# A three-layer fp32 kernel on one core: score matmuls on all four quarters of the array, another opening order, earlier loads and later stores of the first MLP's activations

## The chip, the core and the metric

The kernel runs on one core of a Trainium2 chip. TensorE (PE) multiplies matrices and writes to PSUM, VectorE (DVE) and ScalarE (ACT) work on vectors, GpSimd (POOL) sets up constants, SyncE (SP) issues the DMAs. The metric is the device time of one execution in microseconds.

## The reference, cut to what matters

Windowed attention (4 batches, 8 heads, 576 positions, head size 64, a window of 64 keys), then two MLPs on the 2304 x 512 result. All is float32.

```python
scores = scale * np.matmul(q, k.transpose(0, 1, 3, 2))
mask = (rel >= 0) & (rel < 64)            # rel = query position - key position
scores = np.where(mask, scores, -1000000000.0)
attn = softmax(scores)                     # over the keys
x = np.matmul(attn, v)                     # reshaped to 2304 x 512
h = x @ w_in                               # 512 x 2048
g = np.maximum(h, 0.0) + alpha * np.minimum(h, 0.0)
x = g @ w_out                              # 2048 x 512
h = x @ w_in2
return (h * (1.0 / (1.0 + np.exp(-h)))) @ w_out2
```

## The kernel before

The 2304 tokens are six tiles `t` of 384. An attention **item** `n` is one tile and one pair of heads (24 items; items 0 to 3 are tile 0). An item has six blocks `jb` of 64 queries; each block sees 128 keys. An item takes three steps. `op_s(n, hf)` makes the scores of one half of the item (three blocks): for each block two matmuls, one for each head `e` of the pair. Head `e` lies on partitions 64e to 64e+63 of `qT` and `kT`, and its scores go to the same partitions of PSUM, so the two matmuls of a block use two quarters of the array, rows and columns 0 to 63 and rows and columns 64 to 127. Then DVE scales, masks and takes the row minimum (line 182, three per half), ACT takes the exponential (line 187), and a `flush` on DVE (lines 201 to 203) divides by the row sum. `op_pt(n, hf)` transposes the probabilities on PE and ACT copies them to SBUF as `pt` (line 214). `op_pv(n)` multiplies with V (line 227: the matmuls of the two heads use two column halves of the array, all 128 rows), then ACT and DVE split the result into `xh` and `xl` (lines 232, 233), the left side of the first MLP. A float32 matmul stands as two records in the trace, so the 12 score matmuls of an item are 24 records.

The first MLP's `mlp_h1(t, f)` is 12 matmuls for chunk `f` of 16 (line 317) into one of two PSUM banks `h`; `mlp_g1` has ACT make two relus (lines 324, 325); `join_g1`, one chunk later, adds them on DVE (line 335) and stores the chunk `g` to DRAM (line 338). After all 96 chunks, `load_g1` (line 350) reads them back as `gf`, `split_g1` parts each into `gh` and `gl` (lines 255, 256), and `mlp_o1` is the 12 matmuls of line 369. After that come the second MLP's first layer (line 427) and its second layer (line 504). Weights arrive as 64-bit values: one load, a conversion of three DVE steps (lines 246, 248, 250) and a split (ACT line 255, DVE line 256) for each chunk.

Each engine runs its instructions in the order in which the code issues them. In the opening this order is the string `START`: `q`, `v` load an item, `s`, `t`, `p` are the three steps (`a` and `b` the halves), `w`, `c`, `h` bring weight loads, conversions and splits up to a number, `z` loads alpha, `M` and `G` are `mlp_h1` and `mlp_g1` of tile 0. After it a loop over `t` = 1 to 5 and `f` follows; at `t` = 1 each chunk from `f` = 4 is done for tiles 0 and 1, which below is called a doubled chunk. In the loops up to `t` = 4 an item is handled every four chunks, scores one item ahead.

SP issues all DMAs in code order, so a store that waits for its data holds back the loads behind it. `room(i)` names 40 buffers of 128 x 384 by number; the score buffers `pr` of items 0 to 3 turn over eight rooms, those of later items over four.

## Time and profile before

| | us |
|---|---|
| median of three runs | 886.4 (885.18 to 887.61) |
| profiled execution | 886.67 |
| its span, first to last instruction | 884.9 |
| PE busy | 860.1 |
| PE weight loads busy | 807.8 |
| DVE busy | 495.4 |
| ACT busy | 412.4 |

The span is what the instructions cover; 1.8 us of the execution lie around it. Busy time of PE is the union of its matmul records, whose ends are modelled.

### The profile page before, as it was taken

To read this page: it belongs to the slowest core of one execution; us is meant where nothing else is said; L and a number is where in the kernel's file an instruction comes from. 1 tells how busy PE (TensorE), PEld (TensorE's weight loads), DVE (VectorE), ACT (ScalarE), POOL (GpSimd) and SP (SyncE) were. 2 spreads that over 40 slices of the span, in tenths; PEclk is the share of its full clock that TensorE was granted. 3 is DMA by queue.
4 is the path that set the end of the run, shared out by engine and by line. 5 is a ranking of instruction groups with operands and counts; after the bars stand their busy time and mean duration, and the time that the engine had idled before them with its cause. 6 is when DMAs were issued, how large, how long until landed. Compare 5 with 4: busy or idle time off the path is not lost.

```text
span 884.9 us, 15293 instructions
## 1 busy us (share of the span) xinstructions
PE 860.1 (97%) x5472; PEld 807.8 (91%) x5472; DVE 495.4 (56%) x1223; ACT 412.4 (47%) x1080; POOL 3.8 (0%) x20
## 2 busy tenths in 40 slices
PE   6879999999999999999999999999999999999998
PEld 5769999999999989999999999999999888888886
DVE  6786874567875667757665564554644233233231
ACT  5665656666664543234423355645765222222221
POOL 1000000000000000000000000000000000000000
PEclk9999999999999999999999999999999999999999
DMA  8556634466644556865685345465565443343341
GB/s 262 193 163 214 213 129 137 138 209 208 199 150 174 177 182 218 296 209 160 214 270 155 111 155 179 141 225 180 194 195 171 140 131 107 121 134 121 111 132 56
DMA packets 103468, 152.02 MB, mean 172 GB/s; under 512 B 10336, under 2 KB 87392, under 8 KB 103392
## 3 DMA queue, kind: packets, MB, share of 16 engines
q1 hardware_dynamic: 103392, 151.04, 52.4%
q8 instruction: 43, 0.70, 0.3%
q14 instruction: 33, 0.27, 0.1%
HBM read 99.62 MB, written 51.38 MB: 171 GB/s over the span
## 4 chain that ended last, share of the span: by engine, by line
PE 88%; DVE 5%; ACT 3%; DMA 2%; issue 1%; SPq 0%; ACTq 0%; DVEq 0%
PE acc L504 22%; PE h L317 21%; PE acc L369 21%; PE qa L427 11%; PE qd L427 5%; PE pa L174 3%; PE qb L427 3%; ACT pr L187 2%; PE pa L227 2%; PE pa L212 1%; DMA gf<-g 1%; DVE cva L248 1%; DMA x<-x 1%; DVE pr L203 1%; DVE cva L250 1%
## 5 line engine op out<-in xcount | busy, mean ns | idle before, releaser
L317 PE MATMUL h<-x,i 128*128 128x384 f32 x1152 | 212.2, 339 | 2.1 <-ACT x L232 1.2
L317 PEld LDWEIGHTS h<-x,i 128*128 128x128 f32 x1152 | 198.9, 188 | 6.2 <-issue 2.9
L256 DVE TENSOR_TENSOR gl<-gf,gh 128x384 fp32r<-128x384 f32 x192 | 106.4, 556 | 174.2 <-PE acc L504 122.4
L255 ACT CAST gh<-gf 128x384 fp32r<-128x384 f32 x192 | 97.8, 515 | 212.9 <-PE acc L504 124.8
L369 PE MATMUL acc<-gh,o 128*128 128x384 f32 x768 | 148.9, 335 | 1.8 <-ACT gh L255 1.8
L504 PE MATMUL acc<-o,gh 128*128 128x512 f32 x576 | 147.2, 389 | 0.0
L369 PEld LDWEIGHTS acc<-gh,o 128*128 128x128 f32 x768 | 134.4, 188 | 2.8 <-ACT gh L255 2.8
L504 PEld LDWEIGHTS acc<-o,gh 128*128 128x128 f32 x576 | 108.1, 188 | 22.3
L427 PE MATMUL qa<-v,w2i 128*128 128x384 f32 x576 | 108.2, 334 | 0.6 <-ACT fk L432 0.6
L427 PEld LDWEIGHTS qa<-v,w2i 128*128 128x128 f32 x576 | 100.5, 188 | 1.3 <-ACT fk L432 1.2
L369 PE MATMUL acc<-gl,o 128*128 128x384 f32 x384 | 82.1, 334 | 0.9 <-DVE gl L256 0.9
L324 ACT ACTIVATE a<-h 128x384 f32<-128x384 f32 x96 | 47.0, 489 | 76.3 <-PE h L317 50.3
L504 PE MATMUL acc<-o,gl 128*128 128x512 f32 x288 | 81.9, 389 | 0.0
L335 DVE SCALAR_TENSOR_TENSOR g<-a,nalpha,g 128x384 f32<-128x384 f32 x96 | 58.7, 614 | 33.4 <-ACT g L325 33.3
L187 ACT ACTIVATE pr<-pr,nm 128x128 f32<-128x128 f32 x144 | 56.0, 390 | 38.4 <-DVE nm L182 38.4
L369 PEld LDWEIGHTS acc<-gl,o 128*128 128x128 f32 x384 | 67.9, 188 | 1.2 <-DVE gl L256 1.2
L504 PEld LDWEIGHTS acc<-o,gl 128*128 128x128 f32 x288 | 54.1, 188 | 11.2
L427 PE MATMUL qd<-v,w2i 128*128 128x384 f32 x288 | 57.7, 334 | 0.0
L427 PEld LDWEIGHTS qd<-v,w2i 128*128 128x128 f32 x288 | 50.6, 188 | 0.0
L174 PE MATMUL pa<-kT,qT 64*64 64x128 f32 x576 | 43.6, 304 | 4.7 <-POOL kT L139 3.8
L325 ACT ACTIVATE g<-h 128x384 f32<-128x384 f32 x96 | 46.5, 484 | 0.0
L248 DVE SCALAR_TENSOR_TENSOR cva<-s,cva 128x512 uint32<-128x512 uint32 x64 | 44.3, 693 | 2.2
(64 smaller groups left out, 759.5 us busy)
## 6 DMA issues: line engine op xcount, KB each, us to landing
gf<-g SPq DMA_DIRECT2D x192, 192.0 KB, 2.5
g<-g SPq DMA_DIRECT2D x96, 192.0 KB, 1.9
g<-c SPq DMA_DIRECT2D x96, 192.0 KB, 2.0
s<-in_moe_w_in_dram SPq DMA_DIRECT2D x32, 512.0 KB, 4.6
s<-in_moe_w_out_dram SPq DMA_DIRECT2D x32, 512.0 KB, 4.1
ve<-in_v_dram SPq DMA_DIRECT2D x24, 192.0 KB, 3.4
x<-x SPq DMA_DIRECT2D x24, 192.0 KB, 2.0
xq<-x SPq DMA_DIRECT2D x12, 384.0 KB, 4.5
```

What stands on the lines that cost most here:

```text
L174: nc.tensor.matmul(sc[r, j, :], it["qT"][r, o:o + W], it["kT"][r, o:o + P], start=True, stop=True)
L187: nc.scalar.activation(out=pr[:, j, :], in_=pr[:, j, :], func=AF.Exp, bias=nm[:, j:j + 1], scale=-1.0, accum_out=sm[:, j:j + 1])
L248: nc.vector.scalar_tensor_tensor(out=a, in0=s[:, :, 1], scalar=0xC0000000, in1=a, op0=ALU.bitwise_and, op1=ALU.bitwise_or)
L255: nc.scalar.copy(hi, src)
L256: nc.vector.tensor_tensor(out=lo, in0=src, in1=hi.bitcast(F32), op=ALU.subtract)
L317: nc.tensor.matmul(h, w[:, kk, :], x, start=(kk == 0 and n == 0), stop=(kk == KD - 1 and n == 2))
L324: nc.scalar.activation(out=a, in_=h, func=AF.Relu, scale=-1.0)
L325: nc.scalar.activation(out=g, in_=h, func=AF.Relu)
L335: nc.vector.scalar_tensor_tensor(out=g, in0=a, scalar=nalpha[:, f:f + 1], in1=g, op0=ALU.mult, op1=ALU.add)
L369: nc.tensor.matmul(acc1[t][i], a[:, i * P:(i + 1) * P], b, start=(f == 0 and n == 0), stop=(f == KF - 1 and n == 2))
L427: nc.tensor.matmul(o, w[:, a, k0], b, start=start and kk == 0 and n == 0, stop=kk == 1 and n == 2, skip_group_check=True)
L504: nc.tensor.matmul(acc2[t][i], a[:, i * P:(i + 1) * P], b, start=(f == 0 and n == 0), stop=(f == KF - 1 and n == 2))
```

## The change

- `op_s` issues all 12 score matmuls of an item when its first half is called. Even blocks go to one PSUM bank as before; odd blocks go to a second bank with the two heads' partitions exchanged (`side`), that is to the quarters rows 0 to 63 with columns 64 to 127, and rows 64 to 127 with columns 0 to 63. The halves are now the even and the odd blocks. `op_pv` reads the exchanged columns of `pt`.
- The mask has two block forms where it had four.
- `START` has another order: scores run up to two items ahead of the transposes, the relu and M steps stand elsewhere, and it ends with five weight chunks converted and split where it was six. Items 4 to 7 also take their `pr` from the eight early rooms.
- A chunk's store is issued when three later chunks have been joined.
- At `t` = 5 the first four `load_g1` stand at `f` = 4 to 7 and three splits with three more loads at `f` = 11 to 13; the activation that brings in ACT's Silu table stands at `f` = 0.

```diff
--- before.py
+++ after.py
@@ -18,9 +18,9 @@
 
 
 START = """
-q0 w1 s0a q1 s0b q2 w2 s1a c1 v0 z s1b q3 v1 s2a t0a t0b s2b h1 v2 w3 p0 s3a c2 t1a t1b s3b v3 p1 w4 t2a t2b
-h2 q4 p2 c3 t3a t3b w5 h3 q5 s4a p3 v4 s4b M0 w6 v5 s5a s5b t4a t4b G0 c4 M1 p4 s6a s6b w7 h4 t5a t5b G1 M2 c5 p5
-s7a s7b t6a t6b G2 M3 h5 w8 p6 s8a s8b c6 G3 t7a t7b h6 p7
+q0 w1 s0a q1 q2 s0b w2 s1a v0 s1b c1 q3 s2a v1 z s2b t0a t0b h1 q4 s3a p0 v2 w3 s3b t1a t1b c2 p1 v3 q5 s4a w4 s4b
+t2a t2b h2 v4 p2 s5a w5 s5b t3a t3b v5 p3 c3 w6 s6a t4a t4b s6b M0 p4 h3 G0 c4 s7a t5a t5b s7b M1 p5 w7 G1 h4 t6a t6b
+s8a M2 p6 s8b c5 G2 t7a t7b M3 p7 h5 G3
 """
 
 
@@ -86,17 +86,17 @@
 
     ident = const.tile([P, P], F32, name="ident")
     make_identity(nc, ident)
-    mask = const.tile([P, 4, 2, W], F32, name="mask")
+    mask = const.tile([P, 2, 2, W], F32, name="mask")
     nc.gpsimd.memset(mask, 0.0)
     for e in range(2):
         m = mask[e * W:(e + 1) * W]
         nc.gpsimd.affine_select(
             out=m[:, :, 0, :], in_=m[:, :, 0, :], compare_op=ALU.is_gt, fill=NEG,
-            base=0, pattern=[[0, 4], [1, W]], channel_multiplier=-1,
+            base=0, pattern=[[0, 2], [1, W]], channel_multiplier=-1,
         )
         nc.gpsimd.affine_select(
             out=m[:, :, 1, :], in_=m[:, :, 1, :], compare_op=ALU.is_ge, fill=NEG,
-            base=0, pattern=[[0, 4], [-1, W]], channel_multiplier=1,
+            base=0, pattern=[[0, 2], [-1, W]], channel_multiplier=1,
         )
     nc.gpsimd.memset(mask[:, 0, 0, :], NEG)
     alpha_sb = const.tile([P, KF], F32, name="alpha_sb")
@@ -163,24 +163,31 @@
         nc.sync.dma_start(out=ve, in_=v[t0:t0 + TN, rows].rearrange("(c p) d -> p c d", p=P))
         items[n].update(ve=ve, vo=vo)
 
+    def side(jb, e):
+        x = e ^ jb % 2
+        return slice(x * W, (x + 1) * W)
     def op_s(n, hf):
         it = items[n]
         t = n // NHP
-        sc = att_bank()[:, :HB * P].rearrange("p (b c) -> p b c", b=HB)
-        for j in range(HB):
-            o = (hf * HB + j) * W
-            for e in range(2):
-                r = slice(e * W, (e + 1) * W)
-                nc.tensor.matmul(sc[r, j, :], it["qT"][r, o:o + W], it["kT"][r, o:o + P],
-                                 start=True, stop=True)
-        first = (t * NB + hf * HB) % (S // W) == 0
-        m0 = 0 if first else 1
-        pr = room(turn_early() if n < NHP else turn_pr(), [P, HB, P], F32, "pr")
+        if hf == 0:
+            it["sc"] = [att_bank()[:, :HB * P].rearrange("p (b c) -> p b c", b=HB) for _ in range(2)]
+            for jb in range(NB):
+                o = jb * W
+                for e in range(2):
+                    r = slice(e * W, (e + 1) * W)
+                    nc.tensor.matmul(it["sc"][jb % 2][side(jb, e), jb // 2, :], it["qT"][r, o:o + W],
+                                     it["kT"][r, o:o + P], start=True, stop=True)
+        sc = it["sc"][hf]
+        pr = room(turn_early() if n < EARLY else turn_pr(), [P, HB, P], F32, "pr")
 
         nm = sml.tile([P, HB], F32, name="nm")
         for j in range(HB):
             nc.vector.tensor_tensor_reduce(
-                out=pr[:, j, :], in0=sc[:, j, :], in1=mask[:, m0 + j].rearrange("p u w -> p (u w)"),
+                out=pr[:, j, :], in0=sc[:, j, :],
+                in1=mask[:, min(1, (t * NB + 2 * j + hf) % (S // W))].rearrange("p u w -> p (u w)"),
                 scale=-scale, scalar=3.0e38, op0=ALU.add, op1=ALU.min, accum_out=nm[:, j:j + 1])
         sm = sml.tile([P, HB], F32, name="sm")
         for j in range(HB):
@@ -220,12 +227,12 @@
         t, hp = divmod(n, NHP)
         pb = att_bank()
         for jb in range(NB):
-            hf, j = divmod(jb, HB)
+            j, hf = divmod(jb, 2)
             vt = it["ve"] if jb % 2 else it["vo"]
             for e in range(2):
                 r = slice(e * W, (e + 1) * W)
                 nc.tensor.matmul(pb[r, jb * W:(jb + 1) * W], vt[:, jb // 2, r],
-                                 it[f"pt{hf}"][:, j, r], start=True, stop=True)
+                                 it[f"pt{hf}"][:, j, side(jb, e)], start=True, stop=True)
 
         at = 2 * hp + (32 if t == 2 else 8 * (t % 2))
         xh, xl = (wroom(at + i, [P, TN], F32R, "x") if t == 2 else room(at + i, None, F32R, "x") for i in range(2))
@@ -334,8 +341,17 @@
         t, f, a, g = halves.pop()
         nc.vector.scalar_tensor_tensor(out=g, in0=a, scalar=nalpha[:, f:f + 1], in1=g,
                                        op0=ALU.mult, op1=ALU.add)
-        d = gd1[t, f] = dram.tile([P, TN], F32, name=f"g1_{t}_{f}")
-        nc.sync.dma_start(out=d, in_=g)
+        unstored.append((t, f, g))
+        store_g1(3)
+    unstored = []
+    def store_g1(keep):
+        while len(unstored) > keep:
+            t, f, g = unstored.pop(0)
+            d = gd1[t, f] = dram.tile([P, TN], F32, name=f"g1_{t}_{f}")
+            nc.sync.dma_start(out=d, in_=g)
 
 
     gl1 = {}
@@ -540,6 +556,7 @@
             chunks[done.get(k, 0)][step]()
             done[k] = done.get(k, 0) + 1
 
+    ahead = set()
     for w in START.split():
         x, n = w[0], int(w[1:].rstrip("ab") or 0)
         if x in "qv":
@@ -554,6 +571,7 @@
             upto(in1, "wch".index(x), n)
         else:
             (mlp_h1 if x == "M" else mlp_g1)(0, n)
+            ahead.add(n)
 
 
     LAY3 = NTILE * KF
@@ -633,6 +651,7 @@
         for x in plan.get(g, ()):
             x()
 
+    silu_tables = const.tile([P, 1], F32, name="silu_tables")
 
     for t in range(1, NTILE):
         for f in range(KF):
@@ -648,7 +667,7 @@
                 if f in (2, 6, 10, 13):
                     op_pt(n, 0)
                     op_pt(n, 1)
-            for tt in ((0, 1) if t == 1 and f > 3 else (t,)):
+            for tt in ((0, 1) if t == 1 and f not in ahead else (t,)):
                 mlp_h1(tt, f)
                 mlp_g1(tt, f)
             if t == 1:
@@ -660,17 +679,19 @@
                 upto(out1, 2, x // 3)
                 upto(out1, 1, (x + 1) // 3)
                 upto(out1, 0, (x + 7) // 3)
-            if t == NTILE - 1 and f >= KF - 4:
-                load_g1(f - KF + 4)
-                if f >= KF - 3:
-                    split_g1(f - KF + 3)
-                hook(f - KF)
+            if t == NTILE - 1:
+                if f == 0:
+                    nc.scalar.activation(out=silu_tables, in_=ident[:, :1], func=AF.Silu)
+                if 4 <= f < 8:
+                    load_g1(f - 4)
+                if f >= KF - 5:
+                    split_g1(f - KF + 5) if f < KF - 2 else None
+                    load_g1(f - KF + 9) if f < KF - 2 else None
+                if f >= KF - 4:
+                    hook(f - KF)
     join_g1()
-
-    silu_tables = const.tile([P, 1], F32, name="silu_tables")
-    nc.scalar.activation(out=silu_tables, in_=ident[:, :1], func=AF.Silu)
-    for i in range(4, 7):
-        load_g1(i)
+    store_g1(0)
     for t in range(NTILE):
         for f in range(KF):
             n = t * KF + f
```

Where instructions stand now. First PE at its very start (line 174 before and 181 after are the score matmuls, line 212 and 219 the transposes of item 0, line 227 and 234 its product with V). Before:

```order
L174 MATMUL pa<-kT,qT 64x128 x30
L212 MATMUL pa<-ident,pr 128x128 x6
L174 MATMUL pa<-kT,qT 64x128 x6
L227 MATMUL pa<-pt,vo 64x64 x2
L227 MATMUL pa<-pt,ve 64x64 x2
```

After:

```order
L181 MATMUL pa<-kT,qT 64x128 x36
L219 MATMUL pa<-ident,pr 128x128 x6
L181 MATMUL pa<-kT,qT 64x128 x12
L234 MATMUL pa<-pt,vo 64x64 x2
L234 MATMUL pa<-pt,ve 64x64 x2
```

Before, two and a half items go ahead of the transposes of item 0 and the missing half stands behind them; now three whole items go ahead, and a whole fourth item stands behind.

Second, ACT at the end of the opening, from the copies of item 6's probabilities on (COPY `pt`) to the exponentials of item 9 (the last ACTIVATE `pr`). ACTIVATE `a` and `g` are the relus of an M step, CAST `x` belongs to `op_pv`, CAST `i` to a weight split. Before:

```order
L214 COPY pt<-pa 128x384 x2
L324 ACTIVATE a<-h 128x384
L325 ACTIVATE g<-h 128x384
L255 CAST i_818<-cva 128x512
L232 CAST x<-pa 128x384
L187 ACTIVATE pr,sm<-pr,nm 128x128 x6
L324 ACTIVATE a<-h 128x384
L325 ACTIVATE g<-h 128x384
L214 COPY pt<-pa 128x384 x2
L255 CAST i_912<-cva 128x512
L232 CAST x<-pa 128x384
L187 ACTIVATE pr,sm<-pr,nm 128x128 x6
```

After:

```order
L221 COPY pt<-pa 128x384 x2
L194 ACTIVATE pr,sm<-pr,nm 128x128 x3
L239 CAST x<-pa 128x384
L194 ACTIVATE pr,sm<-pr,nm 128x128 x3
L331 ACTIVATE a<-h 128x384
L332 ACTIVATE g<-h 128x384
L221 COPY pt<-pa 128x384 x2
L239 CAST x<-pa 128x384
L262 CAST i_916<-cva 128x512
L331 ACTIVATE a<-h 128x384
L332 ACTIVATE g<-h 128x384
L194 ACTIVATE pr,sm<-pr,nm 128x128 x6
```

Before, the copies of item 7 (the second COPY) stand behind six exponentials of item 8 and the relus of M3; now the exponentials come in two parts around item 6's cast, the relus of M2 stand ahead of the copies, and those of M3 behind them.

Third, SP at the end of the first MLP's first layer (`g_5_12` is the stored chunk 12 of tile 5, `gf` a chunk read back, `s` a weight load). Before:

```order
L338 DMA g_5_11_4135<-g 128x384
L350 DMA gf<-g_0_0_702 128x384
L241 DMA s_4143<-in_moe_w_in_dram 128x1024
L241 DMA s_4145<-in_moe_w_in_dram 128x1024
L338 DMA g_5_12_4165<-g 128x384
L350 DMA gf<-g_0_1_803 128x384
L338 DMA g_5_13_4191<-g 128x384
L350 DMA gf<-g_0_2_898 128x384
L338 DMA g_5_14_4221<-g 128x384
L350 DMA gf<-g_0_3_999 128x384
L338 DMA g_5_15_4234<-g 128x384
L350 DMA gf<-g_0_4_1184 128x384
```

After:

```order
L354 DMA g_4_15_3923<-g 128x384
L354 DMA g_5_0_3947<-g 128x384
L366 DMA gf<-g_0_0_984 128x384
L354 DMA g_5_1_3969<-g 128x384
L248 DMA s_3975<-in_moe_w_out_dram 128x1024
L366 DMA gf<-g_0_1_1004 128x384
L354 DMA g_5_2_3997<-g 128x384
L366 DMA gf<-g_0_2_1038 128x384
L354 DMA g_5_3_4023<-g 128x384
L366 DMA gf<-g_0_3_1064 128x384
L354 DMA g_5_4_4045<-g 128x384
L248 DMA s_4051<-in_moe_w_out_dram 128x1024
```

Before, the first chunk read back stands behind the store of `g_5_11`; now it stands behind the store of `g_5_0`, and four are read by the store of `g_5_3`.

## Rows read from the trace of the kernel before

**Rows 1.** The page: span, and busy time by engine.

```profile
span 884.9 us, 15293 instructions
PE 860.1 (97%) x5472; PEld 807.8 (91%) x5472; DVE 495.4 (56%) x1223; ACT 412.4 (47%) x1080; POOL 3.8 (0%) x20
```

**Rows 2.** Sums by stretch: length, busy PE, PEld, DVE, ACT, POOL; clock; DMA share, GB/s.

```profile
5.50:60.00 54.50, 41.28 (x469) 34.63 (x465) 43.85 (x192) 36.50 (x144) 0.00 (x0) 0.94 0.69 216
60.00:75.44 15.44, 15.44 (x150) 14.52 (x150) 10.15 (x33) 8.45 (x26) 0.00 (x0) 0.89 0.54 173
75.44:267.00 191.56, 191.30 (x1586) 182.77 (x1586) 134.68 (x413) 119.68 (x370) 0.00 (x0) 1.00 0.54 178
...
61.00:62.00 1.00, 1.00 (x11) 1.00 (x13) 0.81 (x4) 0.51 (x2) 0.00 (x0) 0.50 0.12 46
```

**Rows 3.** PE in order of time: start, us, line, records; in brackets idle before, releaser.

```profile
60.00 0.34 PE L227 MATMUL pa<-pt,vo 128*64 128x64 f32 x4 [3.62 <-ACT pt L214]
...
60.87 2.83 PE L174 MATMUL pa<-kT,qT 64*64 64x128 f32 x24
63.63 4.73 PE L317 MATMUL h<-x,i 128*128 128x384 f32 x24
...
73.14 0.34 PE L227 MATMUL pa<-pt,vo 128*64 128x64 f32 x4
...
73.99 1.53 PE L174 MATMUL pa<-kT,qT 64*64 64x128 f32 x24
75.44 4.80 PE L317 MATMUL h<-x,i 128*128 128x384 f32 x26
```

**Rows 4.** The same view from 73.99 to 74.03 us: the start of that score block.

```profile
73.99 0.33 PE L174 MATMUL pa<-kT,qT 64*64 64x128 f32 x2
```

**Rows 5.** Line 174 from 76 to 305 us: records, duration ns min/median/max, starts.

```profile
L174 PE MATMUL pa<-kT,qT x312: 269/269/320, 93.8 to 251.5; 64*64 64x128 f32 x156
```

**Rows 6.** Waits from 5.5 to 60 us: engine line <- releaser, us, times, longest.

```profile
PE pa L227 <- ACT pt L214: 4.8, 3, 3.6
PE pa L227 <- issue: 4.4, 3, 2.2
```

**Rows 7.** A conversion on DVE (three steps, then the next instruction), and splits, grouped.

```profile
38.50 0.42 DVE L246 TENSOR_SCALAR cva<-s 128x512 uint32<-128x512 uint32 x1
...
40.29 0.16 DVE L201 TENSOR_SCALAR sm<-sm 128x3 f32<-128x3 f32 x1
...
L256 DVE TENSOR_TENSOR i<-cva,i 128x512 fp32r<-128x512 f32 x6 | 4.2, 692 | 4.4 <-ACT i L255 4.4
```

**Rows 8.** ACT in order of time: item 8's first exponential, item 7's copies.

```profile
56.42 0.40 ACT L187 ACTIVATE pr<-pr,nm 128x128 f32<-128x128 f32 x1 [1.94 <-DVE nm L182]
...
59.48 0.84 ACT L214 COPY pt<-pa 128x384 f32<-128x384 f32 x2
```

**Rows 9.** The opening's first microseconds, DVE and PE in order of time.

```profile
5.54 0.29 DVE L182 CUSTOM_DVE_ANT_0 pr<-pa,mask 128x128 f32<-128x128 f32 x1 [5.54 <-PE pa L174]
...
7.60 4.10 PE L174 MATMUL pa<-kT,qT 64*64 64x128 f32 x36 [0.92 <-DMA kT<-in_k_dram]
```

**Rows 10.** PE in order of time where line 369 begins.

```profile
308.03 1.68 PE L369 MATMUL acc<-gh,o 128*128 128x384 f32 x8 [0.60 <-ACT gh L255]
...
313.48 1.68 PE L369 MATMUL acc<-gh,o 128*128 128x384 f32 x8 [0.99 <-ACT gh L255]
```

**Rows 11.** Waits from 296 to 330 us, and SP's own over the span.

```profile
ACT gh L255 <- DMA gf<-g: 11.3, 6, 3.8
...
PE acc L369 <- DVE gl L256: 0.9, 1, 0.9
...
SPq L338 <- DVE g L335: 125.8, 63, 5.2
```

**Rows 12.** ACT in order of time: a relu in the last loop, and the Silu table.

```profile
297.06 0.49 ACT L324 ACTIVATE a<-h 128x384 f32<-128x384 f32 x1 [1.15 <-PE h L317]
...
309.69 1.28 ACT L671 ACT_TABLE_LOAD   x1
```

## The prediction

> **What bounds the kernel now.** I read the busy times first: PE has work for 860.1 of 884.9 us [rows 1], so time is won only where PE's own work shrinks or where PE stands still. The sums by stretch, read second, tell where that is. From 75.44 to 267 us PE is busy for 191.30 of 191.56 us at full clock, DVE for 134.68: there the sum of PE's instructions is the time. In the opening, from 5.5 to 60 us, PE is busy for only 41.28 of 54.50 us and DVE for 43.85, with DMA at 0.69: no engine is full, and the chain runs through DVE, ACT and PE by turns. From 60 to 75.44 us PE is full again, at a mean granted clock of 0.89 [rows 2]. The waits, read third, give the opening's idle time: PE's product with V waits for ACT's copies of the transposed probabilities, 4.8 us, and 4.4 us more behind "issue" [rows 6]. One other place has PE idle: the first chunks of line 369 [rows 10].
>
> **The score matmuls.** In the loop a block of 24 score records takes from 73.99 to 75.44, 1.45 us, until the next MLP matmul starts [rows 3]. In the first 0.03 us two records stand beside each other [rows 4], and the 24 end 1.53 us after the first start, at 0.27 us each [rows 3, 5]: starts spread over 1.26 us in 12 pairs, a pair every 0.105 to 0.11 us. So two quarters work at a time, each at one record per 0.11 us, and two quarters are empty. The change spreads the same 24 records over four quarters, six for each. If all four start together the starts spread over five steps, about 0.6 us; if the second pair always comes one step behind the first, six or seven steps, 0.65 to 0.75 us. The nearest row for the pace is the product with V: also 24 records, two column halves at a time, from 73.14 to 73.99 us, 0.85 us with the change over [rows 3]. I take the new block at 0.90 us, near that row, a saving of 0.55 us per item (0.66 if all start together, 0.45 if the second pair costs two more steps). Rows 5 has 312 records, 13 blocks, behind 76 us, all in stretches where PE is full: 13 x 0.55 = **7.2 us** (5.9 to 8.6). DVE and ACT do the same for each block and are busy for 0.70 and 0.62 of that stretch; they take the tighter pace.
>
> The trace has no record in the two crossed quarters, so that they overlap with the straight ones is the open point. Below, the saving goes to nothing if they do not (rival B) and to a loss if each change between straight and crossed drains the array (rival D). What speaks for overlap: the two records of a pair lie in different rows and different columns [rows 4], and those of line 227 in different columns of the same rows; both kinds of neighbour already run beside each other. What is new is two row halves that write through the same columns; the second PSUM bank is there for that.
>
> A rule of the Trainium skill speaks against it. Row 4 shows the two heads of one block starting together while both write the same PSUM tile `pa`, on different partitions. The Trainium skill, "TensorEngine Tiling (Array Packing)", section "Gotcha 1: PSUM Pressure", says that different row tiles cannot access the same PSUM bank at one time. Taken literally it would already forbid the pair of rows 4, so the trace disagrees with it in that form; read as a limit on how many quarters run at once it is rival B, and the sum would be B's.
>
> **The opening.** Three edits bear on it.
>
> First, less work on DVE: it ends with five chunks converted and split, not six. A conversion takes 40.29 - 38.50 = 1.79 us and a split 0.69 us on DVE [rows 7], 2.5 us that move behind 60 us, where DVE is busy for 10.15 of 15.44 us [rows 2] and has room.
>
> Second, the order on ACT. At 60.00 PE has stood idle for 3.62 us for item 7's copies [rows 3], because they start at 59.48, behind six exponentials of item 8 (from 56.42) and two relus [rows 8]. In the new order three exponentials and the relus of M2 stand ahead of them, and M3, 12 matmuls or some 2.2 us at the pace of rows 3 (4.80 us for 26, the last one's 0.4 us of latency taken off), stands on PE between item 7's transposes and its product. But items 1, 2 and 3 now have their product directly behind their transposes on PE, with the exponentials of a later item ahead of the copies on ACT. What is queued behind those waits is only score work that runs ahead, but each lies on the way of x to the first M. The best case takes all of the 4.8 + 4.4 us [rows 6] half away and the 2.5 us too, some 5 us earlier at the last product; the worst puts one more wait of 3 us, like that of rows 3, into the chain. I take half of the 2.5 us: the last product at 58.8 instead of 60.0, **1.2 us** (5 earlier to 3 later).
>
> Third, what follows it. Behind the 3.62 us idle, item 9's scores ran at a granted clock of 0.50 from 61 us on [rows 2], 60.87 to 63.63, 2.76 us where the warm block takes 1.45 [rows 3]. With M3 just ahead of the product the idle stretch should be about 1 us and the clock stay at its upper level; the block then takes 0.90, 1.86 us less, and item 10's (73.99) 0.55 less. Together **2.4 us**. From 60 us on PE is full [rows 2], so this counts in full.
>
> The rest of the opening I cost at nothing. Item 0's first half now waits for all 12 matmuls and both halves of q and k: DVE starts up to 1 us later than 5.54, but then has both halves of the item, and the next scores wait for item 1's keys until 7.60 in either order [rows 9]; without that cover it would cost that 1 us. The smaller mask shortens POOL's setup, which the same DMA covers. Reading `pr` from eight rooms only removes waits.
>
> **Loads and stores of the first MLP.** Line 369 stands for 0.60 and 0.99 us for `gh` [rows 10] and for 0.9 us for `gl`, and ACT's split waited 11.3 us for `gf` [rows 11]. All three go: the first splits are then done before the loop ends, and seven chunks are loaded. Including the slower first matmul behind each pause that is about **2.9 us** (2.3 to 3.2). The stores: SP spends 125.8 us waiting for DVE's g [rows 11], off PE's path; a store three chunks later only frees its room later, still six chunks of about 2 us ahead of the next writer. Nothing. The Silu table's 1.28 us moves into the last loop, where ACT idles 1.15 us ahead of a relu [rows 12] and PE has the other of two h banks to work in; without that second bank it would cost at most 1.5 us once. Nothing.
>
> **The sum.** The profiled execution took 886.67 us, its span 884.9; the median of the runs is 886.4, so the base is the same within 0.3 us. 886.67 - 7.2 - (1.2 + 2.4) - 2.9 = **873.0 us**.
>
> **The rivals.**
> - A, the forecast: four quarters at once. With the opening's bounds, 867 to 878 us.
> - B: no more than two quarters work at once. The 7.2 us and the 0.55 us of items 9 and 10 stay; 886.67 - 2.9 - 1.2 - 1.3 (item 9's clock) = 881.3 us. For it: no row shows crossed quarters. Against: both kinds of neighbour overlap today.
> - C: the quarters work, but the opening turns its waits round: items 1 to 3 wait directly behind their transposes, the last product comes 3 us later and not 1.2 earlier: 877 us. For it: the exponentials and relus of rows 8 hold ACT for 3 us ahead of one item's copies. Against: DVE has 10 us idle before 60 us to take it up.
> - D, slower: each change between straight and crossed quarters drains the array. The handover from a score block to the full array costs about 0.2 us in rows 3 (1.45 less 1.26). Five changes per block at 0.2 us add 1.0 us to an unshortened 1.45, on 14 blocks on PE's path 14 us: 886.67 + 14 - 2.9 - 1.2 = 896.6 us. It decides for slower from 4.1 / 14 / 5 = 0.06 us per change. For it: two row halves share columns, which is new. Against: the steps from pair to pair show no pause today.
> - E: the score edit gives little and the opening loses about what line 369 gains: within 2.7 us of 886.4.
>
> **How the numbers follow.** A 0.70, B 0.12, C 0.09, D 0.05, E 0.04. The likeliest is A, so 873.0. The range of 867.0 to 881.5 takes in A, C and the most of B. A run of this kernel tells apart some 0.3%, 2.7 us: faster by more has A, B and C, 0.91; within it 0.04; slower 0.05.
>
> **What would show it.** Score blocks of 24 records from first start to the next instruction in about 0.9 us, four records beside each other in the first 0.05 us (A), or 1.45 us with pairs (B), or over 1.6 us (D). Line 174's busy time falls from one block's 1.53 to about 1.0. The first doubled chunk starts at 71.8 us, not 75.44, item 9's scores at the upper clock. No pause at the start of line 369. I am wrong in the opening if the last product with V of item 7 stands later than 60 us, and wrong about line 369 if its first chunks still wait for `gh`.

## The result, and the profile of the changed kernel

The changed kernel takes 878.25 us (median of four runs, 878.11 to 878.33); the kernel before took 887.0 us beside it (885.18 to 888.42). The ratio is 0.9906, with a 95% interval of 0.9887 to 0.9925: faster by 8.8 us or 0.9%, within the stated range, 5.2 us above the predicted 873.0. The profiled execution of the changed kernel took 878.24 us with a span of 876.3, 8.6 less than the 884.9 of [rows 1]. Line numbers of the score, transpose and product matmuls are now 181, 219 and 234, of the first MLP 324 and 385.

The span, cut at three points that both traces have (the start of the first doubled chunk, of line 369 or 385, and of the second MLP's first layer), shows in which stretch the 8.6 us lie and in which stretch the forecast missed:

| us | before | after | change | forecast |
|---|---|---|---|---|
| start to the first doubled chunk | 75.44 | 73.56 | -1.9 | -3.6 |
| first doubled chunk to line 369 / 385 | 229.74 | 226.54 | -3.2 | -7.2 |
| of it PE idle | 0.26 | 4.18 | +3.9 | 0 |
| first MLP's second layer | 203.56 | 200.03 | -3.5 | -2.9 |
| the rest | 376.2 | 376.2 | 0 | 0 |

The page of the changed kernel answers to [rows 1]: PE's busy time falls by 12.8 us, 4.2 more than the span.

```profile
span 876.3 us, 15307 instructions
...
PE 847.3 (97%) x5472; PEld 795.0 (91%) x5472; DVE 495.6 (57%) x1223; ACT 410.7 (47%) x1080; POOL 3.1 (0%) x20
```

The sums by stretch, columns as in [rows 2]. The first is new, from inside the opening; the next two answer to the second and third of [rows 2], and the last is the start of line 385.

```profile
20.00:40.00 20.00, 13.00 (x160) 10.55 (x158) 13.88 (x59) 11.34 (x45) 0.00 (x0) 0.50 0.53 175
60.00:73.56 13.56, 12.93 (x150) 11.87 (x151) 11.56 (x34) 9.78 (x31) 0.00 (x0) 1.00 0.66 206
73.56:267.00 193.44, 189.26 (x1632) 179.46 (x1629) 138.54 (x423) 121.11 (x376) 0.00 (x0) 1.00 0.58 183
300.10:313.10 13.00, 13.00 (x76) 13.00 (x76) 11.67 (x26) 6.67 (x16) 0.00 (x0) 1.00 0.75 243
```

Line 385 starts without a pause, where line 369 paused in [rows 10]. The stretch behind 60 us is at full clock, where it was 0.89. But the loop from 73.56 us, in which PE stood for 0.26 us before, now has 4.2 us of idle time: 193.44 less 189.26. PE's waits from 73.56 to 300.10 us:

```profile
PE h L324 <- ACT g L332: 3.5, 5, 1.1
PE pa L234 <- ACT pt L221: 0.6, 1, 0.6
```

PE in order of time at a score block in the loop, and its first records alone (as [rows 3, 4]):

```profile
93.14 0.89 PE L181 MATMUL pa<-kT,qT 64*64 64x128 f32 x24
93.95 4.45 PE L324 MATMUL h<-x,i 128*128 128x384 f32 x24
99.31 0.98 PE L324 MATMUL h<-x,i 128*128 128x384 f32 x4 [0.90 <-ACT g L332]
...
93.14 0.34 PE L181 MATMUL pa<-kT,qT 64*64 64x128 f32 x4
```

The last line is cut to 93.137 to 93.16 us: four records start within it, where two started in [rows 4]. From the block's first start to the next instruction it is 93.95 - 93.14 = 0.81 us, against 1.45. So the four quarters work at once, and a block is shorter by 0.64 us. The third line shows what happens two chunks later: PE stands for 0.90 us, for ACT.

### The profile page after: what moved, and what is told of

It is laid out like the page before. It is cut to its first block, busy times and chain, and to the rows that moved or that the text cites. A ratio compares the mean times of both kernels' runs of the same rounds, so it can differ in the third digit from the quotient of the medians.

```text
span 876.3 us, 15307 instructions
## 1 busy us (share of the span) xinstructions
PE 847.3 (97%) x5472; PEld 795.0 (91%) x5472; DVE 495.6 (57%) x1223; ACT 410.7 (47%) x1080; POOL 3.1 (0%) x20
## 4 chain that ended last, share of the span: by engine, by line
PE 85%; DVE 5%; ACT 5%; DMA 2%; issue 2%; SPq 0%; ACTq 0%; DVEq 0%
PE acc L520 22%; PE acc L385 22%; PE h L324 17%; PE qa L443 11%; PE qd L443 5%; PE qb L443 3%; ACT pr L194 2%; PE pa L234 2%; PE pa L181 1%; PE pa L219 1%; DMA x<-x 1%; DMA s<-in_moe_w_out_dram 1%; DVE cva L255 1%; DVE pr L210 1%; DVE pr L188 1%
## 5 line engine op out<-in xcount | busy, mean ns | idle before, releaser
L255 DVE SCALAR_TENSOR_TENSOR cva<-s,cva 128x512 uint32<-128x512 uint32 x64 | 44.4, 693 | 2.2
L257 DVE SCALAR_TENSOR_TENSOR cva<-s,cva 128x512 uint32<-128x512 uint32 x64 | 44.3, 692 | 2.2
```

Of the source, the lines that this page charges most:

```text
L255: nc.vector.scalar_tensor_tensor(out=a, in0=s[:, :, 1], scalar=0xC0000000, in1=a, op0=ALU.bitwise_and, op1=ALU.bitwise_or)
L257: nc.vector.scalar_tensor_tensor(out=a, in0=s[:, :, 0], scalar=29, in1=a, op0=ALU.logical_shift_right, op1=ALU.bitwise_or)
```

## The experiments

Each time below is a median, with the range of its runs or its ratio to the kernel before on the same chip and that ratio's 95% interval. My theory from the changed kernel's trace had three parts. One: the score blocks gain 0.64 us each, but DVE and ACT, which work through an item in one piece, now reach PE at several items and give a part back. Two: the new opening is worth about nothing. Three: the loads are worth some 3.5 us and the stores nothing. The rivals: the score blocks are worth less than they look, or the opening cancels a gain of its own by a loss elsewhere.

### The parts apart

The scores alone, in the old opening and with the old loads and stores:

```diff
 # before, with op_s, side, op_pv and the mask of the change
+        if hf == 0: ... 12 score matmuls into two banks, odd blocks with the heads exchanged
+        sc = it["sc"][hf]
+                out=pr[:, j, :], in0=sc[:, j, :],
+                in1=mask[:, min(1, (t * NB + 2 * j + hf) % (S // W))]...
```

> The kernel before with the score change alone (four quarters, both halves' matmuls issued at once, the mask's two forms); the opening's order, the loads and the stores are as before. Theory 1: four quarters overlap, a block takes 0.82 us where it took 1.45 to 1.5, but in the loop ACT's relus stand behind six exponentials and the two h banks run out, so PE waits for ACT there. Then 13 blocks give back 13 x 0.63 = 8.2 us and 3.5 to 5 us of it return as new waits of line 317 for ACT; the two blocks at 60 to 75 us add 1.3 to 1.9 us: about 881 us against 886.9, with at least 3 us of line 317's waits for ACT behind 75 us. Rival 2: those waits come from the weight chunk that the new opening leaves to the loop, or from the late stores. Then they are not here, line 317 waits for less than 1 us, and the time is about 877 us.

It took 882.63 us (880.33 to 883.3), ratio 0.9949 (0.9933 to 0.9965). In its profile, of the run with 880.33 us, the loop is 224.88 us, 4.9 less than before, with 2.50 us of idle PE. The waits of PE in that loop:

```profile
PE h L324 <- ACT g L332: 1.8, 4, 0.9
PE pa L234 <- ACT pt L221: 0.6, 1, 0.6
```

Thirteen blocks at 0.64 us are 8.3 us. The new idle time takes 2.2 of it back, and the rest of what is missing, 1.2 us, is the restart behind each pause: idle time is counted from the modelled end of the last matmul, 0.16 us after the next one would have started (24 records of 4.45 us, each 0.34 us long, start 0.18 us apart), and the first four matmuls behind a pause take 0.98 us where four of line 385 take 0.85. That is some 0.3 us for each pause; this loop has five and the loop before had one, so the four new ones come to some 1.2 us. The expectation was off in two numbers: line 324 waits for ACT for 1.8 us, not 3 or more, and the time is 1.6 us above 881.

The opening alone:

```diff
 # before, with the change's START
-        pr = room(turn_early() if n < NHP else turn_pr(), ...)
+        pr = room(turn_early() if n < EARLY else turn_pr(), ...)
```

> The kernel before with the new opening alone (its order and the eight rooms for items 0 to 7); scores are made in two quarters, half by half, and loads and stores are as before. Theory 1: the new order gains nothing by itself up to item 7's product, since items 1 to 3 wait for ACT's copies directly behind their transposes (the changed kernel's product of item 7 stands at 60.6 us, 60.0 before); it saves the half clock of item 9's scores, 1.3 us, and loses about 0.6 us: 885.5 to 887.5 us. Rival: the new order is worth what was forecast for it without the scores, 2.5 us: 884.4 us.

It took 886.46 us, ratio 0.9994 (0.9979 to 1.0009): no difference that can be measured. Item 7's product starts at 61.25 us, not earlier than the 60.00 of [rows 3], and item 9's scores run at the upper clock:

```profile
61.25 0.34 PE L227 MATMUL pa<-pt,vo 128*64 128x64 f32 x4 [0.32 <-ACT pt L214]
...
62.13 1.53 PE L174 MATMUL pa<-kT,qT 64*64 64x128 f32 x24
```

So the block that took 2.76 us in [rows 3] takes 1.45 here, yet the time stands where it was. In its profile, of the run with 889.38 us, the loop is 232.88 us, 3.1 more than before, with 2.7 us of idle time for ACT's relus. But 2.2 of these are one pause, which ends at 201.33 us, behind a wait of DVE for the first weights of `w_out` (a wait that is taken up below); the other two pauses are 0.26 us each. So little of this loop's 3.1 us is the opening's own.

```profile
PE h L317 <- ACT g L325: 2.7, 3, 2.2
DVE cva L246 <- DMA s<-in_moe_w_out_dram: 6.1, 1, 6.1
```

The loads and stores alone:

```diff
 # before, with the change's load_g1, store_g1 and Silu lines
+        unstored.append((t, f, g))
+        store_g1(3)
...
+                if 4 <= f < 8:
+                    load_g1(f - 4)
```

> The kernel before with the early loads, the late stores and the Silu table's new place alone. Theory 1: the three pauses at the start of line 369 go, 2.9 us, and nothing else changes: 884.0 us. Rival: the late stores or the early loads cost part of it elsewhere (new waits of line 317 or of line 369 later): 885 us or more.

It took 883.29 us, ratio 0.9961 (0.995 to 0.9972): 3.6 us. The first MLP's second layer takes 200.07 us, like the 200.03 of the changed kernel and 3.5 less than before, and it starts without a pause. The sums by stretch at its start:

```profile
305.69:318.69 13.00, 13.00 (x76) 13.00 (x76) 11.66 (x26) 6.67 (x16) 0.00 (x0) 1.00 0.80 264
```

The product of the scores' and the loads' ratios, 0.9949 x 0.9961 = 0.991, is the whole change's 0.9906: the two add, and the opening adds nothing.

### What the quarters do

The same 24 records, with the three straight blocks first and the three crossed ones behind them:

```diff
-            for jb in range(NB):
+            for jb in (0, 2, 4, 1, 3, 5):
```

> The changed kernel with one edit: the 12 score matmuls of an item are issued in the order of blocks 0, 2, 4, 1, 3, 5, so that the straight quarters work first and the crossed ones after them. Work, banks, halves and places are the same. If overlap of all four quarters is what shortens the block, it goes back to 1.4 to 1.5 us, the new waits of line 324 for ACT go too, and the time rises by 13 x 0.63 - 4 = about 4 us to 882 us. If the shorter block comes from something else (two banks, one wait where there were two), it stays at 0.82 us and 878.3 us.

It took 879.79 us, ratio 0.9924 (0.9905 to 0.9943), about 2 us less than expected. PE in order of time, a block and its first 0.29 us (93.37 to 93.66) alone:

```profile
93.37 1.15 PE L181 MATMUL pa<-kT,qT 64*64 64x128 f32 x24
94.45 0.80 PE L324 MATMUL h<-x,i 128*128 128x384 f32 x3
...
93.37 0.61 PE L181 MATMUL pa<-kT,qT 64*64 64x128 f32 x8
```

The block takes 1.08 us, not 1.45: eight records have begun after 0.29 us, where pairs at 0.11 us would give six. The starts of the 24 records make two rows of six pairs, each with a first step of 0.16 us and then steps of 0.11 us: one from 0 to 0.60 us, one from 0.28 to 0.88 us behind the block's first. So the crossed blocks do not wait for the end of the straight ones; they begin after the third of the six straight pairs. Blocks in turn remain the better order by 0.27 us, 13 x 0.27 = 3.5 us; the loop is longer by only 1.9, because the waits for ACT fall from 3.5 to 2.0 us at the same time. That a gain in PE's work here is partly paid with waits for ACT shows from this side too.

### What took the loop's gain back

One of the pauses in order of time, in the changed kernel: DVE from 93.81 us and ACT from 96.09; PE's rows are those above, from 93.14.

```profile
93.81 0.69 DVE L263 TENSOR_TENSOR i<-cva,i 128x512 fp32r<-128x512 f32 x1
94.41 0.16 DVE L208 TENSOR_SCALAR sm<-sm 128x3 f32<-128x3 f32 x1
94.61 0.17 DVE L209 RECIPROCAL rs<-sm 128x3 f32<-128x3 f32 x1
94.82 0.56 DVE L210 TENSOR_TENSOR pr<-pr,rs 128x384 f32<-128x384 f32 x1
95.30 0.55 DVE L240 TENSOR_TENSOR x<-pa,x 128x384 fp32r<-128x384 f32 x1
95.76 0.28 DVE L188 CUSTOM_DVE_ANT_0 pr<-pa,mask 128x128 f32<-128x128 f32 x1
...
96.09 0.40 ACT L194 ACTIVATE pr<-pr,nm 128x128 f32<-128x128 f32 x1 [1.93 <-DVE nm L188]
...
98.42 0.47 ACT L331 ACTIVATE a<-h 128x384 f32<-128x384 f32 x1
98.79 0.47 ACT L332 ACTIVATE g<-h 128x384 f32<-128x384 f32 x1
```

PE goes on to the next chunk at 93.95. DVE first has a weight split, the older item's row sums and the split of x to do, and comes to the masks at 95.76, 1.81 us behind. ACT, idle for 1.93 us, then runs six exponentials in a row and comes to the relus only at 98.42. PE fills both `h` banks in 4.45 us and has no third: it goes on at 99.31, when the first bank is read.

The same place in the kernel before, DVE and PE in order of time, rows not shown ahead of the prediction:

```profile
96.47 0.28 DVE L182 CUSTOM_DVE_ANT_0 pr<-pa,mask 128x128 f32<-128x128 f32 x1
...
95.31 4.46 PE L317 MATMUL h<-x,i 128*128 128x384 f32 x24
100.02 1.15 PE L317 MATMUL h<-x,i 128*128 128x384 f32 x5 [0.26 <-ACT g L325]
```

There the masks came 1.16 us behind the block, 0.65 earlier by that measure, and PE stood for 0.26 us. The block is shorter by 0.64 us, DVE's queue is not, and the pause is longer by 0.64: at this item the whole gain goes into the pause.

If that is so, handling half of an item's vector work one chunk later takes the pauses away, with the same instructions:

```diff
-                if f % 4 == 0 and n + 1 < NI:
-                    op_s(n + 1, 0)
-                    op_s(n + 1, 1)
+                if f % 4 < 2 and n + 1 < NI:
+                    op_s(n + 1, f % 4)
```

> The changed kernel with one edit in the loop: the second half of an item's scores (DVE and ACT only, its matmuls are issued with the first half) is handled one chunk later, so that ACT has three exponentials in a row ahead of the relus where it had six. Theory 1 (PE waits for ACT because six exponentials stand ahead of the relus when the doubled chunks run): the waits of 0.90 us behind 77 and 98 us go, about 2 x 1.2 us with the slower restart, and those of 0.6 and 0.3 us behind 216 and 250 us shrink: 875.5 us. Rival 2 (ACT is simply short of time there): they move by a chunk and stay, 878.3 us. The pause of 1.09 us at 194 us has another cause by theory 1, the late weight load, and need not go.

It took 875.62 us (874.93 to 877.1), ratio 0.9874 (0.9857 to 0.989), and the loop 223.07 us with 1.09 us of idle time. PE's waits in that loop:

```profile
PE pa L234 <- ACT pt L221: 0.6, 1, 0.6
PE h L324 <- ACT g L332: 0.4, 2, 0.2
```

The 3.5 us of waits for the relus are 0.4. It is the item's work in one piece ahead of the relus (six masks on DVE, then six exponentials on ACT) that holds PE, not a lack of time on ACT, which is busy for 121.11 of 193.44 us. The edit parts both, so it doesn't tell the share of the masks from that of the exponentials. The pause at 194 us, which by the expectation need not go, went too.

One of the five pauses, from 194.1 to 195.17 us, has another beginning. DVE stands for the first weights of `w_out`, with an item's masks queued behind:

```profile
186.57 0.43 DVE L253 TENSOR_SCALAR cva<-s 128x512 uint32<-128x512 uint32 x1 [4.23 <-DMA s<-in_moe_w_out_dram]
...
195.17 1.16 PE L324 MATMUL h<-x,i 128*128 128x384 f32 x5 [1.09 <-ACT g L332]
```

The kernel before had the same wait, of 3.0 us, without a pause of PE. Issuing these loads at the end of tile 2 removes it:

```diff
+            elif t == 2:
+                upto(out1, 0, f - 11)
```

> The changed kernel with one edit: the first four loads of the second weight matrix are issued at the end of tile 2 and not at the start of tile 3. In the trace DVE stands for 4.2 us for the first of them, in order, with the next item's scores behind it, and PE pauses for 1.09 us about 8 us later. Theory 1: that pause goes, 1.1 to 1.4 us: 877 us. Rival 2: the pause comes from the six exponentials alone, as the others do; then DVE's wait goes but PE's pause stays, 878.3 us.

It took 876.98 us, ratio 0.9892 (0.9875 to 0.991). DVE has no wait for `w_out` left, and PE's waits for the relus fall from 3.5 to 2.4 us in four pauses. The loop is 225.19 us, 1.4 less than in the changed kernel; the times' intervals overlap, so that the 1.3 us are likely, not shown by the times alone.

### The opening

The products of items 0 to 3 in the changed kernel, PE in order of time. Each is the first of its item:

```profile
17.59 0.48 PE L234 MATMUL pa<-pt,vo 128*64 128x64 f32 x4 [3.42 <-ACT pt L221]
...
24.22 0.48 PE L234 MATMUL pa<-pt,vo 128*64 128x64 f32 x4 [3.45 <-issue]
...
30.62 0.49 PE L234 MATMUL pa<-pt,vo 128*64 128x64 f32 x4 [1.77 <-issue]
...
37.02 0.48 PE L234 MATMUL pa<-pt,vo 128*64 128x64 f32 x4 [1.77 <-issue]
```

They come 6.4 to 6.6 us apart. PE waits for ACT's copies of item n with nothing else queued (item 1's begin at 23.67 us; the row names only "issue"), so the scores of item n + 3, which stand behind that product, start late, and DVE and ACT get them late: one ring through three engines. I put the scores of items 4 to 7 ahead of the product:

```diff
 # START, four scores one product earlier; all else as in the change
-... t1a t1b c2 p1 v3 q5 s4a w4 s4b t2a t2b h2 v4 p2 s5a w5 s5b t3a t3b v5 p3 c3 w6 s6a t4a t4b s6b M0 p4 h3 G0 c4 s7a ...
+... t1a t1b s4a c2 p1 v3 q5 w4 s4b t2a t2b s5a h2 v4 p2 w5 s5b t3a t3b s6a v5 p3 c3 w6 t4a t4b s6b M0 s7a p4 h3 G0 c4 ...
```

> The changed kernel with one edit in the opening: the scores of item n+3 are called ahead of the product of item n, where they stood behind it (items 4 to 7). Theory 1 says the opening lost its gain because PE waits for ACT's copies directly behind the transposes of items 1 to 3, and DVE's and ACT's work on the next scores waits for PE in turn, a ring of 6.4 us per item. With the scores ahead, DVE and ACT have work in that time: the product of item 7 comes 2 to 4 us earlier than 60.6 us, the time falls to 874.5 to 876.5 us. Rival 2: the opening is bound by DVE's own work; then the product stays within 1 us of 60.6 us and the time is 878 us.

It took 876.57 us (875.41 to 877.71), ratio 0.9887 (0.9872 to 0.9902). Items 1 and 2 are now 5.65 us apart, item 7's product starts at 58.58, and the first doubled chunk at 71.56 us:

```profile
25.27 0.48 PE L234 MATMUL pa<-pt,vo 128*64 128x64 f32 x4 [1.96 <-DVE rs L209]
...
30.92 0.48 PE L234 MATMUL pa<-pt,vo 128*64 128x64 f32 x4 [1.02 <-ACT pt L221]
...
58.58 0.34 PE L234 MATMUL pa<-pt,vo 128*64 128x64 f32 x4 [1.60 <-ACT pt L221]
```

That is the opening that the forecast had seen in the change (58.8 and 71.8). The interval of its ratio overlaps that of the changed kernel, so the gain in time is likely and not shown by this run alone. Two more runs weigh the change's own opening. The changed kernel with the old order and the old rooms:

```diff
-q0 w1 s0a q1 q2 s0b w2 s1a v0 s1b c1 q3 ... M3 p7 h5 G3
+q0 w1 s0a q1 s0b q2 w2 s1a c1 v0 z s1b q3 ... G3 t7a t7b h6 p7
...
-        pr = room(turn_early() if n < EARLY else turn_pr(), ...)
+        pr = room(turn_early() if n < NHP else turn_pr(), ...)
```

> The changed kernel with the opening of before (order and rooms); four quarters, loads and stores as changed. It measures what the new opening is worth where scores use four quarters. Theory 1: little, since the product of item 7 comes no earlier; the score change alone and the loads alone gave 0.9949 and 0.9961, together 0.9910, so this kernel takes about 879 us and the opening's part of the change is 1 us or less. Rival: the new opening is worth the 1.9 us by which the first doubled chunk comes earlier in the changed kernel's trace, or more: 880 us or more.

And the changed kernel once more on the same chip:

```diff
 # the changed kernel, nothing edited
```

> The changed kernel as it is, beside the two others on the same chip: 878.3 us, ratio 0.9906, so that the others can be read against it and not only against the kernel before.

They took 879.32 us (878.99 to 881.62; ratio 0.9924, 0.9895 to 0.9953) and 879.1 us (878.2 to 879.96; ratio 0.9914, 0.9892 to 0.9937). The opening makes no difference here either. The traces show the two halves of that zero. In the profiles with the old opening item 7's product starts between 59.83 and 61.87 us (four: the kernel before and three edits), in those with the change's between 60.58 and 62.73 (seven): no earlier. From that product to the first doubled chunk it is 12.98 us in both profiles of the changed kernel, 2.5 less than the 15.44 of [rows 3], as forecast. But the loop behind it is 226.54 and 226.75 us, against 225.19 with the old opening. PE and DVE at the first doubled chunk, in the changed kernel:

```profile
73.56 4.45 PE L324 MATMUL h<-x,i 128*128 128x384 f32 x24
78.92 4.43 PE L324 MATMUL h<-x,i 128*128 128x384 f32 x24 [0.90 <-ACT g L332]
...
73.41 0.69 DVE L263 TENSOR_TENSOR i<-cva,i 128x512 fp32r<-128x512 f32 x1
74.02 0.16 DVE L208 TENSOR_SCALAR sm<-sm 128x3 f32<-128x3 f32 x1
...
75.37 0.28 DVE L188 CUSTOM_DVE_ANT_0 pr<-pa,mask 128x128 f32<-128x128 f32 x1
```

And with the old opening, where that chunk begins at 76.20 us:

```profile
75.18 0.69 DVE L257 SCALAR_TENSOR_TENSOR cva<-s,cva 128x512 uint32<-128x512 uint32 x1
75.79 0.16 DVE L208 TENSOR_SCALAR sm<-sm 128x3 f32<-128x3 f32 x1
...
77.14 0.28 DVE L188 CUSTOM_DVE_ANT_0 pr<-pa,mask 128x128 f32<-128x128 f32 x1
```

The masks begin 1.81 us behind the chunk's start in the changed kernel and 0.94 with the old opening. Of the 0.87 us between them 0.6 to 0.7 are the split at 73.41, for the weight chunk that the new opening leaves over; with the old opening no split stands between conversion and row sums here. In the changed kernel PE stands for 0.90 us at this place, in both profiles (the second at 80.50 us); with the old opening the matmuls run through but for 0.04 us. A part of the loop's difference also stands at the pause that ends at 195.17 us, behind `w_out`: 1.09 and 1.27 us in the two profiles of the changed kernel, 0.54 with the old opening.

### The stores, and all three edits together

The stores at once, as before, in the changed kernel:

```diff
-        store_g1(3)
+        store_g1(0)
```

> The changed kernel with the stores of the first MLP's chunks issued at once again, all else as changed. Theory 1: SP's waits are off the path, no difference beyond 0.5 us: 878 us, with the waits of line 324 for ACT as they are. Rival 3: the late stores crowd the DMA queues behind the weight loads (the store's median landing went from 1.9 to 3.8 us) and are part of the new waits: 877 us or less.

It took 878.68 us, ratio 0.9909 (0.9895 to 0.9924), against the changed kernel's 0.9906: by the time, the late stores are worth nothing by themselves. In this one profile the pause behind `w_out` is 0.21 us and the loop 0.9 to 1.1 us shorter than in the changed kernel's two; but the opening alone, with its stores at once, had 2.2 us there, so whether late stores lengthen that pause stays open. They land later: the median from issue to landing, last column of the DMA issues, first the changed kernel and then this one:

```profile
g<-g SPq DMA_DIRECT2D x96, 192.0 KB, 3.8
```

```profile
g<-g SPq DMA_DIRECT2D x96, 192.0 KB, 1.9
```

Last, the three edits that helped, together:

```diff
 # the changed kernel with the START of the scores one product earlier,
 # the second half of an item one chunk later, and the loads of w_out at the end of tile 2
```

> The changed kernel with the three edits that helped one by one: the second half of an item's scores one chunk later, the scores of item n+3 ahead of the product of item n in the opening, and the first loads of the second weight matrix at the end of tile 2. Theory 1 takes the three for separate waits: 2.6 + 1.7 + 1.3 = 5.6 us less than the changed kernel, 872.7 us. Rival: the waits follow one another, and what one edit frees the next takes: 875 us, no better than the best of them.

It took 872.16 us (871.91 to 872.41), ratio 0.9836 (0.9815 to 0.9857), 6.9 us under the changed kernel on the same chip and 15.2 under the kernel before. Against the run with the stores at once on their chip, which is the changed kernel in time, the three edits gave 3.1, 2.1 and 1.7 us: 6.9 as well. But that the three remove three separate waits isn't shown, and the traces speak against it for the loads of `w_out`. The loop is 223.05 us with 1.09 us of idle time and the same two rows of waits as with the second half later alone, where it is 223.07 us: there DVE already had no wait for `w_out`. What this kernel has beyond that edit lies in the opening: its first doubled chunk starts at 70.34 us, against 75.54 with the second half later, 73.56 and 75.14 in the changed kernel and 71.56 with the scores ahead. So the half later and the scores ahead add; the loads of `w_out` have nothing left to give in this loop, and what the last 1.7 of the 6.9 us are stays open.

## Why the prediction was right and where it was wrong

**Right, the quarters.** The open point, whether crossed and straight quarters overlap, is settled: four records start within 0.02 us, and a block takes 0.81 us. "I take the new block at 0.90 us" was too careful; its bound of "0.66 if all start together" holds. Rivals B and D fall: B's block would be 1.45 us, D's over 1.6. That the 0.90 was careful brought the sum nearer to the result by luck: with 0.81 the loop's term would have been 8.3 us, not 7.2, and the miss 1.1 us larger. The rule of the Trainium skill ("TensorEngine Tiling (Array Packing)", "Gotcha 1: PSUM Pressure") holds in neither form here: each of the two banks is written by two row tiles at once, and four tiles run.

**Wrong, the step that carried them to the end.** "DVE and ACT do the same for each block and are busy for 0.70 and 0.62 of that stretch; they take the tighter pace." The blocks gained 8.3 us, more than the 7.2, and the loop 3.2. A share of busy time says that an engine has room over 190 us; it says nothing of the order in which it serves. At an item's start both have the item's work in one piece ahead of the relus, for two `h` banks that last 4.45 us. The 0.26 us by which PE's busy time fell short of the stretch in [rows 2] were the mark of it: the pause at 100.02 us, where nothing was to spare. Spreading that piece, with the same instructions, gave 3.1 us back. I should have followed those 0.26 us to their row and laid DVE's and ACT's queues of that item beside the 4.45 us.

**Wrong, the opening's start.** "The last product at 58.8 instead of 60.0": it stood at 60.58 and 62.16. The prediction had named this as the mark for being wrong in the opening, and rival C had the cause, "items 1 to 3 wait directly behind their transposes". That measured 3.4, 3.5, 1.8 and 1.8 us, for items 0 to 3. C's time of 877 is the closest to the result, and by A's own bounds, 867 to 878, the 878.25 lies just outside; but C reached its time by other terms, since most of the miss lies in the loop. The range took the result in because it was wide enough for B. The granted clock from 20 to 40 us, where those waits lie, does not order the results: it was 0.50 in the changed kernel's profile and 0.86 in its second one, where the product came later; with the scores ahead it was 0.95, and 0.60 with all three edits, where the product came earliest, at 57.54 us.

**Right, what follows it.** Item 9's scores at the upper clock and both blocks shorter: 2.4 us forecast, 2.5 measured from item 7's product to the first doubled chunk. **Wrong, that DVE had room** behind 60 us for the weight chunk moved there: its split stands ahead of item 10's masks and brings a pause of 0.90 us. Of what the opening gained at 73.56 us the loop gave 1.4 to 1.6 us back, against the loop with the old opening.

**Right, the loads and the stores.** Line 385 starts without a pause; 2.9 us forecast, within 2.3 to 3.2, and 3.5 to 3.6 measured, a little over the bound. The stores and the Silu table cost nothing that the times show. That a late store frees its room "still six chunks of about 2 us ahead of the next writer" did not quite hold: in the second profile of the changed kernel, and in those of four edits that keep the late stores, DVE waits 1.0 to 1.5 us for a store to land, without a pause of PE.

**The sum.** The miss of 5.1 us in the span is 4.0 of the loop and 1.7 of the opening, less 0.6 of the loads.

## What to carry to other kernels

When PE's work in a full stretch shrinks, lay the queue of each engine that frees PE's banks beside the time that those banks last, item by item; busy shares of 0.6 to 0.7 hid 5 us of new pauses and restarts. Independent matmuls of 64 x 64 in four quarters, in turn and into two banks, cut such a block to 0.56 of its time. In an opening that is a ring through three engines, what counts is what stands on PE ahead of the wait, so issue the next item's work before the matmul that waits.

## What the runs showed of the hardware

- A matmul whose quarter is free starts ahead of earlier ones whose quarter is busy, so across quarters PE does not keep strictly to the order that "The kernel before" gives for each engine: with the straight blocks first, the first crossed pair began 0.28 us behind the first straight one, with three of six straight pairs not yet begun, and 24 records took 1.08 us, not 1.45.
- The opening of one and the same kernel differs between executions, here by the granted clock: item 7's product stood at 60.58 and 62.16 us in the two profiles of the changed kernel. Item 5's product starts at 50.84 and 50.89 us, behind 1.75 and 2.37 us of idle PE, and item 6's at 55.85 and 57.44. In between, the clock was at its upper level (2.4 GHz) in the first profile and at the lower one (1.2 GHz) in the second, and the six transposes behind item 5's product took 0.87 and 1.54 us. Of the seven profiles with the change's opening three had 0.50 from 52 to 54 us, with item 7's product at 61.80 to 62.73 us; four had 1.00, with 60.58 to 61.25. The sums of one microsecond in the first and the second profile, columns as in [rows 2]:

```profile
52.00:53.00 1.00, 1.00 (x16) 0.83 (x18) 0.57 (x3) 1.00 (x5) 0.00 (x0) 1.00 0.88 278
```

```profile
52.00:53.00 1.00, 1.00 (x11) 0.88 (x9) 0.52 (x3) 0.93 (x4) 0.00 (x0) 0.50 1.01 352
```

- A pause of PE costs more than its idle time in the trace: some 0.3 us more at each pause of the loop, by the lengths of the loop and the rows at 99.31 us.
